# Tile 0's mean from two engines, and small fillers ahead of the first K projection, in a one-core attention and FFN block

## The chip, the core and the metric

The kernel runs on one core of a Trainium2 chip. The metric is the device time in microseconds, the median of a few runs; lower is better.

## The reference

The input x is 2048 x 512 (bf16). Its rows are normalised (layer norm without weights), and two branches are added to x: linear attention with 32 heads of 16 on the normalised rows, and a SwiGLU FFN with F = 1792, on the same normalised rows.

```python
def layernorm(x, eps=1e-5):
    m = jnp.mean(x, axis=-1, keepdims=True)
    v = jnp.var(x, axis=-1, keepdims=True)
    return (x - m) / jnp.sqrt(v + eps)

xn = layernorm(x)
q, k, v = split(xn @ wqkv)                       # 32 heads of 16
phi = lambda t: jnp.where(t > 0, t + 1, jnp.exp(t)) + 1e-6
kv, z = sum_s phi(k) v, sum_s phi(k)             # per head
attn = (phi(q) @ kv) / (phi(q) @ z + 1e-6) @ wo
ffn = (silu(xn @ w_gate) * (xn @ w_up)) @ w_down
out = x + attn + ffn
```

## The kernel before

The 2048 rows are 16 tiles of 128 rows, and each tile lies on the 128 partitions with its 512 columns along the free dimension. A small class keeps one list of instructions per engine: TensorE (PE), ScalarE (ACT), VectorE (DVE), GpSimd (POOL) and the DMA queue of SyncE (SP). Each operation names what it reads and writes, and the class derives the semaphore waits from that. Every engine runs its list strictly in the order in which the program text adds to it, so the order of calls is the schedule, written out by hand.

A phase at the start brings tiles 0 to 3 to TensorE without waiting for the full normalisation. A tile t is centred (its mean subtracted: `xc_half`, `xc_full`), transposed in 128 x 128 blocks by TensorE (`tp_first(t, h, b)`, two blocks for the half h, into PSUM bank b), and copied out by ScalarE (`tc_first`) into `xcT`. The projections take `xcT` (`proj_part(t, "wk", c, pos)`, one matmul over the 128 rows of chunk c, and `proj_first`), and the factor 1/sqrt(var + eps), called `rstd`, comes in afterwards as the scale of the ACT operations that read the projections: `first_ek` (exponential of K), `first_pk` (Relu of K) and `first_pq` (Q). "K 0" is the K projection of tile 0, four matmuls; "K 1" that of tile 1.

The statistics of a tile are `bns` (L297) and `agg` (L300) on DVE, which leave mean and variance in `mv`; `eps` (L325) adds the epsilon and `rstd_of` (L334) raises to the power -1/2 on POOL. For tile 1 the mean comes from ACT instead: `mean_act` (L305) copies the row scaled by 1/512 with a running sum. `xn_dve` (L314) writes the fully normalised tile `xn`, which the accumulation `gtacc` (L569) and later the DMA transposes for tiles from 4 on (`kproj`, `qproj`, L417) need.

`fill(n, cols)` (L269) issues n matmuls of constants into bank 3, which is overwritten later; they compute nothing. The x and wk loads are issued first by SP and ACT: x 0 by SP, x 1 by ACT, wk 0 and 1 together by SP, wk 3 by ACT, wk 2 by SP. K 0 takes its chunks in the order 0, 1, 3, 2.

The rest of the program follows in loops: tiles 5 to 15 of K and Q with their features and `gtacc`, then 56 steps of the FFN (L770) with the attention's normalisation and the output tiles (L942, L953) between them. The waits on which the steps around the change depend can be read in the lines that follow.

Of the kernel before, what the change touches and what calls it, by code (L numbers as in the profile page):

```python
# [6 lines left out]
ACT = mybir.ActivationFunctionType  # L7
ALU = mybir.AluOpType
AX = mybir.AxisListType

P = 128
S = 2048
D = 512
# [95 lines left out]
def bass_parallel_sum__linear_attn_block__swiglu_ffn__prompt_kernel(  # L109
# [12 lines left out]
    K = _Prog()  # L122
    pe, act, dve, pool, sp = nc.tensor, nc.scalar, nc.vector, nc.gpsimd, nc.sync
    bf, f32 = dt.bfloat16, dt.float32

    with contextlib.ExitStack() as es:
        E = es.enter_context

        def sb(name, shape, d=bf):
            return E(nc.sbuf_tensor(name, [P] + shape, d))  # L130

        x_sb = sb("x_sb", [NT, D])
        xn_sb = sb("xn_sb", [NT, D])
        xc_sb = sb("xc_sb", [4, D])
# [12 lines left out]
        mv = sb("mv", [NT, 2], f32)  # L147
        vpe = sb("vpe", [NT], f32)
        rstd = sb("rstd", [NT], f32)
        nb = sb("nb", [NT], f32)  # L150
# [3 lines left out]
        warm = sb("warm", [1], f32)  # L154
        mact = sb("mact", [2, 1], f32)
        scr = sb("scr", [D])
        pkq = sb("pkq", [NT, 2, D])
        zacc = sb("zacc", [D], f32)
        zhi = sb("zhi", [D])
# [30 lines left out]
        def bk(i):  # L190
            return ("bank", i)
# [31 lines left out]
        def whalf(name, dst, src, h):  # L223
# [16 lines left out]
                out=ident[:, :], in_=ident[:, :], compare_op=ALU.not_equal, fill=1.0,  # L240
                base=0, pattern=[[-1, P]], channel_multiplier=1,
            ),
            r=[("ident",)], w=[("ident",)],
# [19 lines left out]
        cx = nc.const_aps.tensor(1.0, (P, 512), bf)  # L263

        def fill(n, cols, after=()):
            K.op(
                "pe",
                [
                    (lambda: pe.matmul(banks[3][:, 0:cols], cw, cx[:, 0:cols], start=True, stop=True))  # L269
                    for _ in range(n)  # L270
                ],
                r=list(after), w=[bk(3)],
            )
# [22 lines left out]
        def bns(t):  # L296
            K.op("dve", lambda: dve.bn_stats(stats[:, t, :], x_sb[:, t, :]), r=[("x", t)], w=[("st", t)])  # L297

        def agg(t):
            K.op("dve", lambda: dve.bn_aggr(mv[:, t, :], stats[:, t, :]), r=[("st", t)], w=[("mv", t)])  # L300

        def mean_act(t):
            K.op(
                "act",
                lambda: act.activation(  # L305
                    scr[:, :], x_sb[:, t, :], ACT.Copy, scale=1.0 / D, accum_out=mact[:, t, :],
                ),
                r=[("x", t)], w=[("mact", t), ("scr",)],
            )

        def xn_dve(t):
            K.op(
                "dve",
                lambda: dve.tensor_scalar(  # L314
                    out=xn_sb[:, t, :], in0=x_sb[:, t, :], scalar1=mv[:, t, 0:1], scalar2=rstd[:, t:t + 1],
                    op0=ALU.subtract, op1=ALU.mult,
                ),
                r=[("x", t), ("mv", t), ("rstd", t)], w=[("xn", t)],
            )

        def eps(t, eng):
            h = dve if eng == "dve" else pool
            K.op(
                eng,
                lambda: h.tensor_scalar(  # L325
                    out=vpe[:, t:t + 1], in0=mv[:, t, 1:2], scalar1=1e-5, scalar2=None, op0=ALU.add,
                ),
                r=[("mv", t)], w=[("vpe", t)],
            )

        def rstd_of(t):
            K.op(
                "pool",
                lambda: pool.tensor_tensor(out=rstd[:, t:t + 1], in0=vpe[:, t:t + 1], in1=nhalf[:, :], op=ALU.pow),  # L334
                r=[("vpe", t), ("nhalf",)], w=[("rstd", t)],
            )
# [15 lines left out]
            )  # L352

        HD = D // 2

        def xc_half(t, h, mean=None, dep="mv"):
            mean = mv[:, t, 0:1] if mean is None else mean

            K.op(
                "dve",  # L360
                lambda: dve.tensor_scalar(
                    out=xc_sb[:, t, h * HD:(h + 1) * HD], in0=x_sb[:, t, h * HD:(h + 1) * HD],
                    scalar1=mean, scalar2=None, op0=ALU.subtract,
                ),
                r=[("x", t), (dep, t)], w=[("xc", t, h)],
            )

        def xc_full(t):
            K.op(
                "dve",  # L370
                lambda: dve.tensor_scalar(
                    out=xc_sb[:, t, :], in0=x_sb[:, t, :], scalar1=mv[:, t, 0:1], scalar2=None, op0=ALU.subtract,
                ),
                r=[("x", t), ("mv", t)], w=[("xc", t, 0), ("xc", t, 1)],
            )
# [8 lines left out]
        def tp_first(t, h, b):  # L384
            tb = banks[b].bitcast(bf)[:, 0:HD].rearrange("p (c s) -> p c s", c=2)
            K.op(
                "pe",
                [
                    (lambda c=c: pe.transpose(  # L389
                        tb[:, c, :], xc_sb[:, t, (2 * h + c) * P:(2 * h + c + 1) * P], ident[:, :],  # L390
                    ))
                    for c in range(2)
                ],
                r=[("xc", t, h), ("ident",)], w=[bk(b)],
            )

        def tc_first(t, h, b):
            tb = banks[b].bitcast(bf)[:, 0:HD].rearrange("p (c s) -> p c s", c=2)
            K.op(
                "act",  # L400
                lambda: act.activation(xcT[:, NDC * t + 2 * h:NDC * t + 2 * h + 2, :], tb, ACT.Copy),
                r=[bk(b)], w=[("xcT", t, h)],
            )
# [36 lines left out]
        def proj_part(t, wname, c, pos):  # L440
            lo, b = (D, kb(t)) if wname == "wk" else (0, qb(t))
            K.op(
                "pe",
                lambda: pe.matmul(  # L444
                    banks[b], xcT[:, NDC * t + c, :], wqkv_sb[:, c, lo:lo + D],
                    start=(pos == 0), stop=(pos == NDC - 1),
                ),
                r=[("xcT", t, c // 2), (wname, c)], w=[bk(b)],
            )

        def kb(t):
            return 2 * (t % 2)

        def qb(t):
            return 2 * (t % 2) + 1
# [49 lines left out]
        def first_pk(t):  # L505
            K.op(
                "act", lambda: act.activation(kpos[:, t % NE, :], banks[kb(t)], ACT.Relu, scale=rstd[:, t:t + 1]),
                r=[bk(kb(t)), ("rstd", t)], w=[("kpos", t % NE)],
            )
# [74 lines left out]
        def xn(t):  # L584
            xn_dve(t)
            if t >= 3:
                transpose_dma(t)

        fill(8, 512)
        bns(0)  # L590
        agg(0)
        xc_half(0, 0)
        xc_half(0, 1)
        mean_act(1)
        xc_half(1, 0, mact[:, 1, :], "mact")
        xc_half(1, 1, mact[:, 1, :], "mact")
        tp_first(0, 0, 4)
        tc_first(0, 0, 4)
        fill(1, P)
        tp_first(0, 1, 5)  # L600
        tc_first(0, 1, 5)
        eps(0, "pool")
        tp_first(1, 0, 6)
        tc_first(1, 0, 6)
        bns(1)
        rstd_of(0)
        xn_dve(0)
        tp_first(1, 1, 7)
        agg(1)
        tc_first(1, 1, 7)  # L610
        bns(2)
        agg(2)
        xc_half(2, 0)
        xc_half(2, 1)
        bns(3)
        agg(3)
        proj_part(0, "wk", 0, 0)
        proj_part(0, "wk", 1, 1)
        proj_part(0, "wk", 3, 2)
        proj_part(0, "wk", 2, 3)  # L620
        first_ek(0)
# [13 lines left out]
        proj_part(0, "wq", 0, 0)  # L635
        proj_part(0, "wq", 1, 1)
        first_pk(0)
        tp_first(2, 0, 4)
        tc_first(2, 0, 4)
        tp_first(2, 1, 5)  # L640
# [26 lines left out]
        xn(4)  # L667
        xload("sp", sp, 12, 2)
        xn_dve(1)
        rstd_of(3)  # L670
        eps(5, "pool")
# [378 lines left out]
```

## Time and profile before

| | us |
|---|---|
| median of 3 runs | 211.25 |
| lowest and highest | 211.05, 211.78 |
| profiled execution, device time | 211.43 |
| its span, first to last instruction | 210.1 |
| PE busy in the span | 206.3 |
| DVE, ACT, POOL busy | 119.6, 70.9, 75.0 |

The profile is of one execution. Its span lies inside the device time, with 1.33 us around it. Lines such as L389 are lines of the kernel; a group's line can be that of a helper that many calls share. PE is TensorE's matmuls and transposes, PEld its weight loads, which overlap matmuls. In a chain of waits each row has a start, a duration, and what ran or what was waited for; in the timeline a row with "xN" is N instructions in a row, from the first one's start to the last one's end.

### The profile page before, as it was taken

The page shows a single profiled execution, that of the slowest core. Times are in us where ns is not written, and L with a number is a line of the kernel's source. Part 1 is how long each engine was busy: PE and PEld are TensorE (multiplying, and loading weights), DVE is VectorE, ACT ScalarE, POOL GpSimd, SP SyncE. Part 2 cuts the span into 40 slices and gives each one's busy share as a digit, 9 for nine tenths or more (in the row PEclk, how much of TensorE's full clock was granted, in tenths as well). Part 3 has the DMA queues.
Part 4 walks back from the last instruction along what each step waited for, and adds up shares of the span by engine and source line. Part 5 has one row for each costly group of instructions (what it writes and reads, how often), then busy time and mean ns, then how long its engine had stood idle before and what let it go on. Part 6 is the DMA issues. An engine that isn't in the chain of part 4 may idle for free.

```text
span 210.1 us, 2753 instructions
## 1 busy us (share of the span) xinstructions
PE 206.3 (98%) x968; PEld 95.3 (45%) x987; DVE 119.6 (57%) x245; ACT 70.9 (34%) x125; POOL 75.0 (36%) x96
## 2 busy tenths in 40 slices
PE   8999999999999999999999999999999999999996
PEld 3444444445444444444444444444444444444444
DVE  3999888335265774647365746365556535374122
ACT  4787666966643331303122312213031213121000
POOL 3667977658032444222140432230424032221200
PEclk9999999999999999999999999999999999999999
DMA  6775444894792011110202110202021010210201
GB/s 196 221 188 122 77 100 100 251 368 156 207 352 48 8 29 27 36 25 28 50 2 50 25 28 25 50 0 50 3 50 25 27 25 28 43 33 27 50 25 53
DMA packets 30287, 16.84 MB, mean 80 GB/s; under 512 B 20928, under 2 KB 29632, under 8 KB 30272
## 3 DMA queue, kind: packets, MB, share of 16 engines
q1 hardware_dynamic: 29984, 16.39, 29.2%
q10 hardware_dynamic: 288, 0.26, 0.4%
q8 instruction: 8, 0.13, 0.3%
q14 instruction: 7, 0.06, 0.1%
HBM read 9.70 MB, written 2.10 MB: 56 GB/s over the span
## 4 chain that ended last, share of the span: by engine, by line
PE 96%; DVE 1%; issue 1%; POOL 1%; DVEq 0%
PE psum L770 44%; PE psum L953 23%; PE psum L417 10%; PE psum L942 7%; PE psum L569 7%; PE psum L444 2%; PE psum L269 2%; PE psum L431 2%; PE psum L389 1%; POOL prod L900 1%; PE psum L868 0%; PE psum L891 0%; DVE pkq L493 0%; DVE den L908 0%; DVE xn_sb L791 0%
## 5 line engine op out<-in xcount | busy, mean ns | idle before, releaser
L785 ACT ACTIVATE sg<-psum 128x512 bf16<-128x512 f32 x56 | 33.4, 598 | 106.8 <-PE psum L770 104.1
L770 PE MATMUL psum<-xnT,wg_sb 128*128 128x512 bf16 x222 | 57.4, 379 | 0.1
L770 PE MATMUL psum<-xnT,wu_sb 128*128 128x512 bf16 x217 | 56.0, 379 | 0.4
L900 POOL TENSOR_TENSOR prod<-pkq,zb 128x512 f32<-128x512 bf16 x16 | 18.6, 1161 | 57.8 <-DVE pkq L493 57.8
L770 PEld LDWEIGHTS psum<-xnT,wu_sb 128*128 128x128 bf16 x224 | 21.9, 98 | 26.4
L770 PEld LDWEIGHTS psum<-xnT,wg_sb 128*128 128x128 bf16 x224 | 21.9, 98 | 26.2
L966 DVE TENSOR_TENSOR out_sb<-psum,x_sb 128x512 bf16<-128x512 f32 (+2 forms) x17 | 11.2, 661 | 36.3 <-PE psum L953 36.3
L924 POOL TENSOR_TENSOR pqn<-pkq,rden 128x512 bf16<-128x512 bf16 x16 | 16.9, 1056 | 36.6 <-DVE rden L918 36.6
L791 DVE TENSOR_TENSOR pkq<-psum,sg 128x512 bf16<-128x512 f32 x28 | 19.2, 687 | 18.5 <-PE psum L770 14.0
L791 DVE TENSOR_TENSOR xn_sb<-psum,sg 128x512 bf16<-128x512 f32 x28 | 18.9, 673 | 13.8 <-PE psum L770 13.2
L953 PE MATMUL psum<-wd_sb,xn_sb 128*128 128x512 bf16 (+2 forms) x123 | 25.4, 355 | 0.2
L953 PE MATMUL psum<-wd_sb,pkq 128*128 128x512 bf16 x110 | 25.2, 379 | 0.1
L417 PE MATMUL psum<-wqkv_sb,xnT 128*128 128x512 bf16 x94 | 22.2, 379 | 0.1
L561 POOL TENSOR_TENSOR zacc<-zacc,pkq 128x512 f32<-128x512 f32 x15 | 17.3, 1156 | 5.0 <-DVE ek L484 4.6
L953 PEld LDWEIGHTS psum<-wd_sb,xn_sb 128*128 128x128 bf16 x126 | 11.8, 98 | 12.5
L953 PEld LDWEIGHTS psum<-wd_sb,pkq 128*128 128x128 bf16 x112 | 11.0, 98 | 13.2
L942 PE MATMUL psum<-m_sb,eq 128*128 128x512 bf16 (+2 forms) x67 | 16.5, 366 | 0.1
L569 PE MATMUL psum<-pkq,xn_sb 128*128 128x512 bf16 x63 | 15.9, 379 | 0.1
L417 PEld LDWEIGHTS psum<-wqkv_sb,xnT 128*128 128x128 bf16 x96 | 9.4, 98 | 11.3
L908 DVE TENSOR_REDUCE den<-prod 128x32 f32<-128x512 f32 x16 | 10.9, 684 | 5.7 <-POOL prod L900 5.7
L297 DVE BATCH_NORM_STATS2 stats<-x_sb 128x6 f32<-128x512 bf16 x16 | 10.9, 681 | 3.2 <-DMA x_sb<-in_A_x_dram 3.2
L493 DVE SCALAR_TENSOR_TENSOR pkq<-pkq,eq 128x512 bf16<-128x512 bf16 x16 | 11.1, 693 | 0.6
(65 smaller groups left out, 142.5 us busy)
## 6 DMA issues: line engine op xcount, KB each, us to landing
out_dram<-out_sb SPq DMA_DIRECT2D x15, 128.0 KB, 1.7
wg_sb<-in_B_w_gate_dram SPq DMA_DIRECT2D x2, 896.0 KB, 7.8
wu_sb<-in_B_w_up_dram SPq DMA_DIRECT2D x2, 896.0 KB, 6.0
wd_sb<-in_B_w_down_dram SPq DMA_DIRECT2D x1, 1792.0 KB, 9.7
x_sb<-in_A_x_dram SPq DMA_DIRECT2D x5, 256.0 KB, 3.0
x_sb<-in_A_x_dram SPq DMA_DIRECT2D x5, 128.0 KB, 3.5
wqkv_sb<-in_A_wqkv_dram SPq DMA_DIRECT2D x5, 128.0 KB, 3.6
wqkv_sb<-in_A_wqkv_dram SPq DMA_DIRECT2D x1, 512.0 KB, 7.9
```

The costliest lines, as they stand in the source:

```text
L417: (lambda c=c: pe.matmul(banks[b], xnT[:, c, t * P:(t + 1) * P], wqkv_sb[:, c, lo:lo + D], start=(c == 0), stop=(c == NDC - 1),))
L493: lambda: dve.scalar_tensor_tensor(out=dst, in0=src, scalar=0.0, in1=e, op0=ALU.max, op1=ALU.add,),
L561: lambda: pool.tensor_tensor(out=zacc[:, :], in0=zacc[:, :], in1=pk, op=ALU.add),
L569: (lambda c=c: pe.matmul(banks[4 + c], xn_sb[:, t, c * P:(c + 1) * P], pkq[:, t, 0, :], start=(t == 0), stop=(t == NT - 1),))
L770: (lambda c=c: pe.matmul(banks[b], w_sb[:, c, fc * P:(fc + 1) * P], xnT[:, c, C * 512:(C + 1) * 512], start=(c == 0), stop=(c == NDC - 1),))
L785: lambda: act.activation(sg[:, j % NSG, :], banks[gb], ACT.Silu),
L791: lambda: dve.tensor_tensor(out=hT(C, fc), in0=banks[ub], in1=sg[:, j % NSG, :], op=ALU.mult,),
L900: lambda: pool.tensor_tensor(out=p, in0=pkq[:, t, 1, :], in1=zb[:, :], op=ALU.mult),
L924: lambda: pool.tensor_tensor(out=pqn[:, t % NPN, :].rearrange("p (h e) -> p h e", e=DH), in0=pkq[:, t, 1, :].rearrange("p (h e) -> p h e", ...
L942: (lambda g=g: pe.matmul(dst, pqnT(t)[:, g, :], m_sb[:, g, lo:hi], start=(g == 0), stop=False,))
L953: (lambda fc=fc: pe.matmul(dst, hT(C, fc)[:, jj * P:(jj + 1) * P], wd_sb[:, fc, lo:hi], start=False, stop=(fc == NFC - 1),))
L966: lambda: dve.tensor_tensor(out=o, in0=src, in1=x_sb[:, t, lo:hi], op=ALU.add),
```

## The change

Tile 0's mean no longer comes from `bns` and `agg`. `mean_parts(0)` sums the first 256 columns on DVE (a multiply by ones with a sum) and the other 256 on ACT, each scaled by 1/512, and `xc_two` subtracts both parts in one DVE instruction with two scalars. `bns(0)` follows the centring of tile 0, and `agg(0)`, `eps(0)` (now on DVE), `rstd_of(0)` and a new `negmean(0)` on POOL (minus mean times rstd) follow the centring of tile 1. Tile 0 is normalised on ACT (`xn_act(0)`) behind `first_pk(0)`, in place of `xn_dve(0)` on DVE.

On PE, the eight fillers of 512 columns become seven and one of 128. The filler of 128 columns between tile 0's two transposes goes away, and four of 128 stand behind them. Tile 1's transposes move from ahead of K 0 to between its second and third matmul. Tile 2 is centred in one instruction instead of two halves.

```diff
+        scr2 = sb("scr2", [D // 2])
+        mpart = sb("mpart", [2], f32)
...
+        def negmean(t):
+            K.op(
+                "pool",
+                lambda: pool.tensor_scalar(
+                    out=nb[:, t:t + 1], in0=mv[:, t, 0:1], scalar1=rstd[:, t:t + 1], scalar2=-1.0,
+                    op0=ALU.mult, op1=ALU.mult,
+                ),
+                r=[("mv", t), ("rstd", t)], w=[("nb", t)],
+            )
+
+        def xn_act(t):
+            K.op(
+                "act",
+                lambda: act.activation(
+                    xn_sb[:, t, :], x_sb[:, t, :], ACT.Identity, scale=rstd[:, t:t + 1], bias=nb[:, t:t + 1],
+                ),
+                r=[("x", t), ("nb", t), ("rstd", t)], w=[("xn", t)],
+            )
...
+        def mean_parts(t):
+            K.op(
+                "dve",
+                lambda: dve.tensor_tensor_reduce(
+                    out=scr2[:, :], in0=x_sb[:, t, 0:HD], in1=cx[:, 0:HD], scale=1.0 / D, scalar=0.0,
+                    op0=ALU.mult, op1=ALU.add, accum_out=mpart[:, 0:1],
+                ),
+                r=[("x", t)], w=[("mpa", t), ("scr2",)],
+            )
+            K.op(
+                "act",
+                lambda: act.activation(
+                    scr[:, 0:HD], x_sb[:, t, HD:D], ACT.Copy, scale=1.0 / D, accum_out=mpart[:, 1:2],
+                ),
+                r=[("x", t)], w=[("mpb", t), ("scr",)],
+            )
+
+        def xc_two(t, h):
+            K.op(
+                "dve",
+                lambda: dve.tensor_scalar(
+                    out=xc_sb[:, t, h * HD:(h + 1) * HD], in0=x_sb[:, t, h * HD:(h + 1) * HD],
+                    scalar1=mpart[:, 0:1], scalar2=mpart[:, 1:2], op0=ALU.subtract, op1=ALU.subtract,
+                ),
+                r=[("x", t), ("mpa", t), ("mpb", t)], w=[("xc", t, h)],
+            )
...
-        fill(8, 512)
+        fill(7, 512)
+        fill(1, P)
+        mean_parts(0)
+        mean_act(1)
+        xc_two(0, 0)
+        xc_two(0, 1)
         bns(0)
-        agg(0)
-        xc_half(0, 0)
-        xc_half(0, 1)
-        mean_act(1)
         xc_half(1, 0, mact[:, 1, :], "mact")
         xc_half(1, 1, mact[:, 1, :], "mact")
+        agg(0)
+        eps(0, "dve")
+        rstd_of(0)
+        negmean(0)
         tp_first(0, 0, 4)
         tc_first(0, 0, 4)
-        fill(1, P)
         tp_first(0, 1, 5)
         tc_first(0, 1, 5)
-        eps(0, "pool")
-        tp_first(1, 0, 6)
-        tc_first(1, 0, 6)
+        fill(4, P)
         bns(1)
-        rstd_of(0)
-        xn_dve(0)
-        tp_first(1, 1, 7)
         agg(1)
-        tc_first(1, 1, 7)
         bns(2)
         agg(2)
-        xc_half(2, 0)
-        xc_half(2, 1)
+        xc_full(2)
         bns(3)
         agg(3)
         proj_part(0, "wk", 0, 0)
         proj_part(0, "wk", 1, 1)
+        tp_first(1, 0, 6)
+        tc_first(1, 0, 6)
+        tp_first(1, 1, 7)
+        tc_first(1, 1, 7)
         proj_part(0, "wk", 3, 2)
         proj_part(0, "wk", 2, 3)
         first_ek(0)
...
         proj_part(0, "wq", 0, 0)
         proj_part(0, "wq", 1, 1)
         first_pk(0)
+        xn_act(0)
         tp_first(2, 0, 4)
```

## The prediction

> **What bounds the kernel now.** I read the page's first part, then the chain of waits for the first 18 us, because every line of the diff lies there.
>
> ```profile
> PE 206.3 (98%) x968; PEld 95.3 (45%) x987; DVE 119.6 (57%) x245; ACT 70.9 (34%) x125; POOL 75.0 (36%) x96
> ...
> PE 96%; DVE 1%; issue 1%; POOL 1%; DVEq 0%
> ```
>
> TensorE is busy 206.3 of 210.1 us and carries 96% of the chain. So an edit ahead of K 0 changes the end only by the moment from which PE has dense work, by pauses it opens after that moment, and by the rate of the matmuls.
>
> ```profile
> 0.84 3.57 PE psum L269 x8
> 4.41 0.03 issue
> 4.44 0.40 PE psum L389 x2
> 4.84 0.11 PE psum L269
> 4.94 0.64 PE psum L389 x6
> 5.58 2.90 PE psum L444 x12
> 8.48 0.22 PE psum L389 x4
> 8.71 0.86 PE psum L444 x4
> ```
>
> The chain (start, us, what) has eight filler matmuls (L269), tile 0's first two transposes at 4.44 (L389), one small filler, six more transposes, then the projections (L444). From 4.44 on there is no pause: the transposes of tile 1 fill the time in which tile 0's transposed halves are copied out and the weights land.
>
> ```profile
> 3.15 0.69 DVE L297 BATCH_NORM_STATS2 stats<-x_sb 128x6 f32<-128x512 bf16 x1 [3.15 <-DMA x_sb<-in_A_x_dram]
> 3.45 0.63 ACT L305 ACTIVATE scr<-x_sb 128x512 bf16<-128x512 bf16 x1 [1.16 <-DMA x_sb<-in_A_x_dram]
> 3.88 0.18 DVE L300 BATCH_NORM_AGGREGATE mv<-stats 128x2 f32<-128x6 f32 x1
> 3.99 0.19 ACT L305 ACTIVATION_READ_ACCUMULATOR scr<-x_sb 128x1 f32 x1
> 4.10 0.48 DVE L361 TENSOR_SCALAR xc_sb<-x_sb,mv 128x256 bf16<-128x256 bf16 x2
> 4.87 1.25 ACT L401 ACTIVATE xcT<-psum 128x256 bf16<-128x256 bf16 x4 [0.70 <-PE psum L389]
> 5.38 1.17 PE L444 MATMUL psum<-wqkv_sb,xcT 128*128 128x512 bf16 x3
> 6.60 1.03 PE L444 MATMUL psum<-wqkv_sb,xcT 128*128 128x512 bf16 x4
> ```
>
> The timeline gives tile 0's path: its load at 3.15, statistics, aggregate, centring, transposes, copies, K 0 at 5.38. The last two rows show the rate: eight fillers start (3.57 - 0.63) / 7 = 0.42 us apart, the four matmuls from 6.60 start (1.03 - 0.38) / 3 = 0.217 apart. K 0's three starts are 5.38, 5.80 and 6.16; the second gap of 0.36 splits into 0.42 and 0.217 rates at about 6.1 us. So up to 6.1 us PE runs at half rate. (PEclk is 9 in all slices, so this is not in the granted clock's row.)
>
> The landing rows of the wk transfers, for the one issued at 1.26 by SP and the one at 1.35 by ACT:
>
> ```profile
> DMA to landing us min/median/max: 3.8/3.8/3.8
> DMA to landing us min/median/max: 3.8/4.0/4.3
> ```
>
> wk 0 and 1 are there at 1.26 + 3.8 = 5.06, wk 3 at 1.35 + 4.3 = 5.65. K 0 can't start before 5.06, whatever tile 0 does. At most 5.38 - 5.06 = 0.32 us is to be had at K 0's start.
>
> **The change part by part.**
>
> *Tile 0's mean.* Statistics, aggregate and wait take 4.10 - 3.15 = 0.95 us to the first centring. Now ACT sums one half: its 128x512 row is 0.63 with the read starting 0.54 after it; the 128x256 ACT row (L401) is 0.38, so the read starts about 0.32 after 3.15 and takes 0.19: 3.66. DVE's half is an operation that the trace does not have. Bounds: not under a 256-wide TENSOR_SCALAR (0.28), and not over the 512-wide statistics plus a read of an accumulator as on ACT (0.69 + 0.19 = 0.88). I take 0.45, nearer the low end, because it passes half as many elements as the 0.69 row. Then mpart is complete at 3.66, and the first centring starts at 3.70 instead of 4.10. With a second scalar it is dearer: the 512-wide rows are 0.40 with two (L314) and 0.35 with one (L371), so 0.28 + 0.05 = 0.33 each. Halves done at 4.05 and 4.29, before at 4.38 and 4.58.
>
> *Tile 0's transposes and copies.* Before, a copy started 4.87 - 4.44 = 0.43 after the first transpose. Now 4.10 + 0.43 = 4.53 and 4.35 + 0.45 = 4.80; ACT is free, since mean_act(1) waits for the read at 3.66 (it writes the same scr) and ends near 3.70 + 0.73 = 4.43. Each copy takes 0.38: halves 4.91 and 5.19. K 0's first matmul: the wk landing 5.06 plus a weight load, about 5.15, 0.22 earlier than 5.38. At the upper bound of DVE's half, the first centring starts at 4.07, K 0 again near 5.38, and this gain is nothing. The four small fillers behind tile 0's transposes need 4 x 0.107 = 0.43 (the chain's one is 0.11), 4.56 to 4.98, inside the wait for wk. They cost nothing there; at the upper bound they still end by 5.35.
>
> *Tile 1's transposes leave the wait and go behind K 0's first pair.* That is what costs. Before, they were done in time that had nothing else in it. Now four transposes, 0.107 each at half rate and 0.055 at full (the chain's 0.22 for 4 at 8.48), stand in dense work. K 0's pair goes 5.15 to 6.00; the transposes 6.00 to 6.27 with the step at 6.1; K 0's second pair starts 6.27 and ends 6.70, where before K 1 started at 6.60. wk 3 (5.65) is long there. Net so far: +0.10.
>
> *K 1 now waits for ACT.* Its first matmul needs tile 1's first half: transposes at 6.00 and 6.10, copy from about 6.37 to 6.75, weight load, matmul near 6.87. Between none (full rate earlier) and 0.3 (half rate, copies late) I take 0.15. Net: K 1 at 6.85 instead of 6.60, +0.25.
>
> *DVE, POOL, xn 0.* bns(0) now stands ahead of tile 1's centring (ready near 5.26, needed at 6.00), and agg(0), eps(0) behind it. rstd(0) needs 5.35 + 0.05 + 0.14 + 0.65 (L334 row), about 6.2; first_ek(0) needs it near 6.92, so 0.7 covers it. negmean on POOL (0.32, the L325 row) delays rstd(2) by at most that, and its first reader, first_ek(2), is at 11.69, rstd(2) at 8.03. Removing xn_dve(0) takes 0.31 from DVE ahead of bns(2), which waited for its transfer to 6.06 anyway; later DVE steps come about 0.2 later and feed xc 3's transposing DMA (from 8.78 to about 9.0, landing 2.5 later, PE needs it at 11.9) and xn 1, 2. xn_act(0) on ACT is 0.63 behind first_pk(0), 8.1 to 8.7. Queued behind it is the copy of tile 2, which in the old order starts at 8.63 and here no sooner than 8.9, because PE is late by 0.25. Without that cover it would cost up to 0.5. gtacc(0) needs xn 0 at 11.1. All at nothing.
>
> *Sum.* K 0's start -0.22, transposes and their place +0.32, K 1's wait +0.15: +0.25 us, carried by dense PE work to the end. The profiled execution took 211.43 (span 210.1, 1.33 around it), 0.18 over the median 211.25. So 211.68 against the former, **211.5** against the latter.
>
> **A rule on the rate.** In the trace the rate steps up at 6.1 us, 5.25 us after the first filler and 1.7 after the last pause (4.41). [...]
>
> **The rivals.**
>
> *The rate steps up later (slower).* The new order has up to three pauses ahead of K 0, near 3.95 to 4.10, 4.2 to 4.3 and 4.98 to 5.15, where the old has 0.03. If the step counts from the last pause, it comes at 5.15 + 1.7 = 6.85: 0.75 x (1 - 0.217 / 0.42) = +0.36, so 211.9. If dense work must start anew, 5.15 + 5.25 = 10.4: 4.3 x 0.48 = +2.1, so 213.6. Against it: PE stays over 85% busy there. It decides over 0.3% from a step at 6.9 on. [...]
>
> *K 0's start is the end's start (faster).* If tile 1's transposes cover a wait for wk 3, and ACT's copies come in time, the gain of 0.22 to 0.32 stays: 210.95 to 211.05. For it speaks only that wk landings vary; here c 3 waited for nothing at 6.16.
>
> *The rate steps up earlier (faster).* At K 0's start, 5.15 rather than 6.1: 0.95 x 0.48 = -0.46, 211.05. To be 0.3% faster it must come before tile 0's transposes, which no row suggests.
>
> *It does nothing measurable.* DVE's half sum is so slow, or wk so late, that PE's order alone decides: 211.25.
>
> **How the numbers follow.** Forecast (+0.1 to +0.5) 0.5, nothing 0.1, faster start 0.1, late step 0.24 (0.1 of it by a whole window or more), early step or a saving I don't see 0.06. A measurement of this kernel tells about 0.3%, 0.63 us, from no change; the three runs alone spread 0.73. Slower beyond that takes most of the late step and the upper ends of the forecast: 0.26. Faster: the last case and part of the faster start: 0.11. Range 210.7 to 212.6: it leaves out the dear end of the late step and the far faster end. The likeliest case alone: 211.3 to 211.8.
>
> **What would show it.** Right: centring from 3.7, K 0's first matmul at 5.1 to 5.2, four transposes between K 0's pairs, K 1 near 6.85 with a weight load released by ACT xcT, nothing new behind 9 us. Wrong: matmul starts 0.42 apart beyond 6.9, DVE's half sum over 0.9 us, K 1 before 6.6, or a pause of PE behind xn_act(0).

## The result, and the profile after

The changed kernel took 211.44 us (median of 22 runs, 210.95 to 211.91), the kernel before, run beside it, 210.99 (22 runs, 210.82 to 211.78). The ratio of the two is 1.0018 with a 95% interval of 1.0010 to 1.0025: 0.2% slower, less than 0.3%, and real. The profiled execution of the changed kernel took 211.51 with a span of 210.3; before's was 211.43 with 210.1.

The page's first part and its chain of waits answer to the first lines of the prediction:

```profile
PE 207.3 (99%) x990; PEld 95.0 (45%) x990; DVE 119.4 (57%) x246; ACT 72.0 (34%) x128; POOL 75.5 (36%) x96
...
PE 90%; POOL 4%; DVE 3%; DMA 1%; issue 1%; ACT 0%; DVEq 0%; POOLq 0%
```

The busy time of PE can't be compared closely, since the trace of before lacks 19 of its 987 matmul records (its weight loads are all there, 987, and the new order has three fillers more). The chain can: PE carried 96% of it, now 90, and POOL and DVE hold 7%. Something on those two engines has come onto the path: the chain now leaves PE at a wait near 20 us and follows POOL and DVE back from there. The 7% is the length of that stretch, not what the change costs.

The timeline of tile 0's path (start, duration, engine, line, operation, and in brackets the engine's idle time before it):

```profile
3.35 0.42 ACT L388 ACTIVATE scr<-x_sb 128x256 bf16<-128x256 bf16 x1 [1.06 <-DMA x_sb<-in_A_x_dram]
3.35 0.43 DVE L380 CUSTOM_DVE_ANT_0 scr<-x_sb,const-bfloat16-1.0 128x256 bf16<-128x256 bf16 x1 [3.35 <-DMA x_sb<-in_A_x_dram]
...
3.67 0.19 ACT L388 ACTIVATION_READ_ACCUMULATOR scr<-x_sb 128x1 f32 x1
3.70 0.08 DVE L380 DVE_READ_ACCUMULATOR2_ANT mpart<- 128x1 f32 x1
...
3.90 0.60 DVE L397 TENSOR_SCALAR xc_sb<-x_sb,mpart 128x256 bf16<-128x256 bf16 x2
...
5.17 0.61 PE L492 MATMUL psum<-wqkv_sb,xcT 128*128 128x512 bf16 x2
...
5.62 0.39 PE L437 MATMUL psum<-ident,xc_sb 128*128 128x128 bf16 x4
...
5.84 1.35 PE L492 MATMUL psum<-wqkv_sb,xcT 128*128 128x512 bf16 x5
...
6.36 0.11 PEld L492 LDWEIGHTS psum<-wqkv_sb,xcT 128*128 128x128 bf16 x2 [0.42 <-ACT xcT L449]
```

The load landed at 3.35, 0.2 later than in the trace of before. Both half sums start then, and the centring follows 0.55 later (before 0.95). K 0's first pair starts at 5.17 and 5.40, tile 1's transposes stand behind it at 5.62, and K 1 starts at 6.37, 0.095 late for ACT's copy (the gap to it is 0.311 where 0.216 is the spacing). The rate has stepped up by 5.17: the last small fillers were still 0.107 apart, the transposes are 0.056 apart. In the trace of before it stepped at 6.1.

So at 6.4 us this execution is 0.23 *ahead* of before's profile, and it stays 0.22 ahead up to 16.7. Then PE pauses twice, here in its timeline:

```profile
16.53 0.59 PE L465 MATMUL psum<-wqkv_sb,xnT 128*128 128x512 bf16 x2
17.11 1.04 PE L617 MATMUL psum<-pkq,xn_sb 128*128 128x512 bf16 x4
17.98 1.89 PE L465 MATMUL psum<-wqkv_sb,xnT 128*128 128x512 bf16 x8
19.98 0.39 PE L617 MATMUL psum<-pkq,xn_sb 128*128 128x512 bf16 x1
```

L617 is `gtacc`. `gtacc(3)` starts at 17.11, 0.366 after the matmul before it, a pause of 0.15. `gtacc(4)` starts at 19.98, 0.27 late. The two take 0.42, the lead of 0.22 becomes a lag of 0.2, and that holds to the end. The list of PEld's waits from 6 to 30 us names what was late (total, times, longest):

```profile
PEld psum L617 <- DVE pkq L541: 0.6, 1, 0.6
PEld psum L492 <- ACT xcT L449: 0.6, 2, 0.4
PEld psum L617 <- DVE xn_sb L335: 0.5, 1, 0.5
```

The DVE rows that it points to, from the timeline of DVE:

```profile
16.65 0.41 DVE L335 TENSOR_SCALAR xn_sb<-x_sb,mv,rstd 128x512 bf16<-128x512 bf16 x1
...
19.24 0.68 DVE L541 SCALAR_TENSOR_TENSOR pkq<-psum,ek 128x512 bf16<-128x512 f32 x1
```

The same two in the trace of before:

```profile
15.88 0.41 DVE L314 TENSOR_SCALAR xn_sb<-x_sb,mv,rstd 128x512 bf16<-128x512 bf16 x1
...
18.48 0.68 DVE L493 SCALAR_TENSOR_TENSOR pkq<-psum,ek 128x512 bf16<-128x512 f32 x1
```

They start at 15.88 and 18.48: DVE is 0.77 late. Going back along DVE's list, it had stood idle twice for POOL:

```profile
14.45 0.41 DVE L335 TENSOR_SCALAR xn_sb<-x_sb,mv,rstd 128x512 bf16<-128x512 bf16 x1 [0.46 <-POOL rstd L355]
15.32 0.41 DVE L335 TENSOR_SCALAR xn_sb<-x_sb,mv,rstd 128x512 bf16<-128x512 bf16 x1 [0.46 <-POOL rstd L355]
```

POOL's rows for tile 5's `eps` and `rstd`, of the changed kernel and then of the kernel before:

```profile
12.00 1.14 POOL L346 TENSOR_SCALAR vpe<-mv 128x1 f32<-128x1 f32 x1
13.22 1.19 POOL L355 TENSOR_TENSOR rstd<-vpe,nhalf 128x1 f32<-128x1 f32 x1
```

```profile
11.37 0.22 POOL L325 TENSOR_SCALAR vpe<-mv 128x1 f32<-128x1 f32 x1
11.68 0.57 POOL L334 TENSOR_TENSOR rstd<-vpe,nhalf 128x1 f32<-128x1 f32 x1
```

POOL's whole chain is later (`eps(2)` at 7.46 for 7.06, its feature product at 9.46 for 8.88), and then `eps(5)`, 0.22 before, took 1.14. This is a chain that the prediction put at nothing.

### The profile page after: what moved, and what is told of

It is laid out like the page before. It is cut to its first block, busy times and chain, and to the rows that moved or that the text cites. A ratio compares the mean times of both kernels' runs of the same rounds, so it can differ in the third digit from the quotient of the medians.

```text
span 210.3 us, 2785 instructions
## 1 busy us (share of the span) xinstructions
PE 207.3 (99%) x990; PEld 95.0 (45%) x990; DVE 119.4 (57%) x246; ACT 72.0 (34%) x128; POOL 75.5 (36%) x96
## 4 chain that ended last, share of the span: by engine, by line
PE 90%; POOL 4%; DVE 3%; DMA 1%; issue 1%; ACT 0%; DVEq 0%; POOLq 0%
PE psum L820 46%; PE psum L1003 23%; PE psum L465 8%; PE psum L992 7%; PE psum L617 5%; POOL rstd L355 2%; DMA x_sb<-in_A_x_dram 1%; POOL vpe L346 1%; DVE stats L299 1%; POOL pkq L574 1%; PE psum L918 0%; PE psum L941 0%; DVE xn_sb L335 0%; DVE pkq L541 0%; DVE pkq L581 0%
## 5 line engine op out<-in xcount | busy, mean ns | idle before, releaser
L820 PE MATMUL psum<-xnT,wu_sb 128*128 128x512 bf16 x224 | 57.5, 379 | 0.0
L617 PE MATMUL psum<-pkq,xn_sb 128*128 128x512 bf16 x64 | 16.0, 379 | 0.1
L355 POOL TENSOR_TENSOR rstd<-vpe,nhalf 128x1 f32<-128x1 f32 x16 | 10.0, 627 | 5.4 <-DVE vpe L346 4.2
```

The costliest lines, as they stand in the source:

```text
L617: (lambda c=c: pe.matmul(banks[4 + c], xn_sb[:, t, c * P:(c + 1) * P], pkq[:, t, 0, :], start=(t == 0), stop=(t == NT - 1),))
L820: (lambda c=c: pe.matmul(banks[b], w_sb[:, c, fc * P:(fc + 1) * P], xnT[:, c, C * 512:(C + 1) * 512], start=(c == 0), stop=(c == NDC - 1),))
```

## The experiments

Theory 1: the order on DVE delays the statistics, POOL's chain comes late, and PE waits at `gtacc`. Theory 2: PE's own order costs the time (tile 1's transposes in dense work, K 1 behind ACT's copy). Beside both stands the moment of the rate step, which differed by 0.95 us between the two profiles.

**The kernel before, again** (unchanged).

> The kernel before, unchanged, for a second profile of it. Theory 1 (POOL): the 22 runs of before lie mostly at 210.8 to 211.1, below the profiled one at 211.43, so this execution should take about 211.0 and its matmul rate should step up before 6.1 us, near 5.2 as in the changed kernel's profile; K 1 then starts near 6.1 instead of 6.60, and TensorE has no new pause up to 25 us. Theory 2 (the order on TensorE): the step comes at 6.1 again, K 1 at 6.60, 211.4.

211.55 in a single execution, beside a median of 210.94 for 29 others of the same kernel. The step came at 6.5, K 1 at 6.85, no pause behind it. The early step that was expected did not come; the step moves from execution to execution of one kernel (6.1 in the first profile, 6.5 here).

**Tile 5's and 6's `eps` taken from POOL** (changed kernel).

```diff
 bns(6)
 agg(6)
+eps(5, "dve")
+eps(6, "dve")
...
 rstd_of(3)
-eps(5, "pool")
 rstd_of(5)
-eps(6, "pool")
 rstd_of(6)
```

> The changed kernel with the two small steps eps(5) and eps(6) on VectorE (0.14 us each) instead of POOL, where eps(5) took 1.14 us in the changed kernel's profile. Theory 1: what the change costs is a late POOL chain (rstd 5 and 6 late, so xn 5 and xn 6, so tile 3's features, so TensorE's waits of 0.15 and 0.27 us at gtacc(3) and gtacc(4)); taking the 1.14 us step away gives 0.25 to 0.45 back: 211.0 to 211.2, and the two waits go. Theory 2: the cost is tile 1's transposes behind K 0 and K 1's wait for ACT, which stay: 211.4, as the changed kernel.

211.32 (12 runs), ratio to before 1.0010 (1.0000 to 1.0021). Neither pause at `gtacc` is in the trace. That alone doesn't show that the edit took them away: tile 0's load was on time here (3.13), and the second profile of the changed kernel itself, with such a load (the last run below), has no such pause either. And its profile took 211.47, because another pause of 0.63 stands at tile 7's K projection:

```profile
23.42 0.81 PE L465 MATMUL psum<-wqkv_sb,xnT 128*128 128x512 bf16 x3 [0.47 <-DMA xnT<-xn_sb]
```

The DMA that transposes tile 7's `xn` needed 5.0 us to land; in most other executions it took 2.4 to 3.8.

**Only PE's part of the change** (kernel before).

```diff
-fill(8, 512)
+fill(7, 512)
+fill(1, P)
...
-fill(1, P)
 tp_first(0, 1, 5)
 tc_first(0, 1, 5)
+fill(4, P)
-tp_first(1, 0, 6); tc_first(1, 0, 6); tp_first(1, 1, 7); tc_first(1, 1, 7)
...
 proj_part(0, "wk", 1, 1)
+tp_first(1, 0, 6); tc_first(1, 0, 6); tp_first(1, 1, 7); tc_first(1, 1, 7)
 proj_part(0, "wk", 3, 2)
```

> The kernel before with TensorE's part of the change alone: seven fillers and a small one, no filler between tile 0's transposes, four small ones behind them, tile 1's transposes between K 0's second and third matmul. Mean, statistics and normalisation stay as before. Theory 1: 211.0, at most 211.1, since POOL and VectorE are untouched. Theory 2: K 1 waits for ACT's copy and tile 1's transposes are in dense work, +0.25: 211.2 to 211.3.

211.42 (12 runs), ratio 1.0019 (1.0007 to 1.0031): without the earlier K 0, PE's order alone costs about as much as the whole change, within this interval. Its timeline and its list of waits:

```profile
5.47 0.60 PE L444 MATMUL psum<-wqkv_sb,xcT 128*128 128x512 bf16 x2
5.92 0.39 PE L389 MATMUL psum<-ident,xc_sb 128*128 128x128 bf16 x4
6.14 1.35 PE L444 MATMUL psum<-wqkv_sb,xcT 128*128 128x512 bf16 x5
```

```profile
PEld psum L444 <- ACT xcT L401: 0.6, 2, 0.4
```

K 0 to K 1 is 1.19 us (5.47 to 6.67), with 0.096 of it K 1's wait, and there is no later pause. K 0 itself is at 5.47, with its load 0.16 later than in before's first profile. Theory 2 is right about its part. (K 0 to K 1 is 0.88 in the old order at full rate, as a run below shows.)

**POOL late without the rest** (kernel before, two spare 128x1 multiplies on POOL that nothing reads).

```diff
 first_pq(0)
+spare(2)
+spare(2)
 eps(2, "pool")
```

> The kernel before with two spare 128x1 operations on POOL ahead of eps(2), which nothing reads: POOL's chain of small steps runs some 0.6 us later, as in the changed kernel, and nothing else is changed. Theory 1: the same collision and the same waits at gtacc(3) and gtacc(4): +0.3 to +0.5, 211.3 to 211.5. Theory 2: POOL has slack, 211.0.

211.29 (12 runs), ratio 1.0011 (0.9999 to 1.0023). In the trace tile 3's features are 0.59 late, PE pauses by 0.12 at `gtacc(0)` and 0.10 at `gtacc(4)`, not at `gtacc(3)`:

```profile
PEld psum L579 <- POOL pkq L536: 0.5, 1, 0.5
PEld psum L579 <- DVE pkq L503: 0.4, 1, 0.4
```

A later POOL chain alone opens pauses of this kind, smaller than the 0.3 to 0.5 that was expected; its effect on the time can't be told from none by this interval.

**Tile 1's transposes back ahead of K 0** (changed kernel).

```diff
+xc_half(1, 0, ...); xc_half(1, 1, ...)
 bns(0)
-xc_half(1, 0, ...); xc_half(1, 1, ...)
 agg(0)
...
 tc_first(0, 1, 5)
-fill(4, P)
+tp_first(1, 0, 6); tc_first(1, 0, 6); tp_first(1, 1, 7); tc_first(1, 1, 7)
...
 proj_part(0, "wk", 1, 1)
-tp_first(1, 0, 6); tc_first(1, 0, 6); tp_first(1, 1, 7); tc_first(1, 1, 7)
```

> The changed kernel with tile 1's four transposes back ahead of K 0 (and its centring ahead of bns(0), so that they are ready in time); the four small fillers behind tile 0's transposes make way for them. Theory 2 (the order on TensorE): K 0 to K 1 again in 0.86 us instead of 1.20, so -0.3 against the changed kernel: 211.1 or less. Theory 1 (late statistics and POOL): statistics come 0.3 later still than in the changed kernel, and waits at gtacc(3) and gtacc(4) take back what K 0 gains: 211.4.

211.41 (9 runs) beside 211.10 of before (27 runs), ratio 1.0017 (1.0007 to 1.0026). K 1 does come earlier, at 5.95, but PE then pauses by 0.29 at 7.46 for tile 2's centring on DVE, by 0.23 at 11.44, and by 0.28 at tile 7's K projection. The gain is given back.

**The same, and `eps` 5 and 6 on DVE** (the diff above and that of tile 5's and 6's `eps`).

> The same, and eps(5) and eps(6) on VectorE as before in the study. If both theories hold, each for a part, this one loses neither: 210.8 to 210.9, the fastest so far. Theory 2 alone: as the run without this edit. Theory 1 alone: as the changed kernel with eps(5), eps(6) moved, 211.3.

211.25 (11 runs), 1.0010 (1.0001 to 1.0020). K 1 at 5.77; pauses of 0.31, 0.22 and 0.10, the first again for tile 2's centring:

```profile
PEld psum L437 <- DVE xc_sb L419: 0.6, 1, 0.6
```

**Tile 0 normalised on DVE again** (changed kernel).

```diff
 rstd_of(0)
-negmean(0)
...
 bns(1)
+xn_dve(0)
 agg(1)
...
 first_pk(0)
-xn_act(0)
```

> The changed kernel with tile 0 normalised on VectorE as before (xn_dve(0) ahead of agg(1), no negmean, no xn_act). Theory 1: VectorE's statistics get 0.3 us later, POOL's chain with them, and TensorE's waits at gtacc(3), gtacc(4) grow: 211.6 to 211.8. Theory 2: TensorE's order is the changed kernel's, 211.4.

211.64 (5 runs, 211.52 to 212.04), ratio 1.0033 (1.0021 to 1.0045), the dearest of all. The load is on time here (3.13); one more row of 0.41 on DVE ahead of tile 2's statistics makes tile 3's features 0.88 late, `eps(5)` on POOL takes 1.14 again, and PE's list of waits begins with the three lines of the changed kernel's first profile, word for word:

```profile
PEld psum L617 <- DVE pkq L541: 0.6, 1, 0.6
PEld psum L492 <- ACT xcT L449: 0.6, 2, 0.4
PEld psum L617 <- DVE xn_sb L335: 0.5, 1, 0.5
```

Theory 1's mechanism is shown: later statistics, the same two pauses (0.21 and 0.27), and a longer time in the median. And `xn_act` seems to be a part of the change that helps (1.0018 with it against 1.0033, with intervals that just overlap).

**No small fillers** (changed kernel without its `fill(1, P)` and `fill(4, P)`).

> The changed kernel without any small filler (the one behind the seven and the four ahead of K 0). If the small fillers hold the time at which the matmul rate steps up, as the rival of a later step has it, the step moves behind 6.9 us in some runs and the median goes up by 0.3 or more, 211.8. If they only fill a pause: 211.4, with the same spread as the changed kernel, 210.95 to 211.9.

Median 211.41 (12 runs), ratio 1.0025 (1.0003 to 1.0047), but two of the 12, which widen this interval, took 213.16 and 213.40. No run of any other kernel here, some 230 in all, was over 212.04. The profiled execution is one of the usual ones:

```profile
4.10 0.65 PE L437 MATMUL psum<-ident,xc_sb 128*128 128x128 bf16 x4
4.97 1.04 PE L492 MATMUL psum<-wqkv_sb,xcT 128*128 128x512 bf16 x2 [0.22 <-ACT xcT L449]
5.80 0.63 PE L437 MATMUL psum<-ident,xc_sb 128*128 128x128 bf16 x4
6.22 1.15 PE L492 MATMUL psum<-wqkv_sb,xcT 128*128 128x512 bf16 x4
```

Here K 0's pair is 0.40 apart and the transposes 0.107: half rate up to 6.3. The two dear runs left no trace; their 1.7 to 2.0 us over the median are near the 2.1 at which the prediction priced a rate step that has to start anew.

**Relieved order** (changed kernel; `eps` 5 and 6 on DVE in their old places, tile 2's statistics and centring ahead of tile 1's statistics).

```diff
-eps(5, "pool")
+eps(5, "dve")
...
-eps(6, "pool")
+eps(6, "dve")
...
-bns(1); agg(1)
 bns(2); agg(2)
 xc_full(2)
+bns(1); agg(1)
```

> The changed kernel with its order on TensorE, but with eps(5) and eps(6) on VectorE where they stand, and tile 2's statistics and centring ahead of tile 1's statistics. Theory 1 (late statistics and POOL are the whole cost): the waits at gtacc(3) and gtacc(4) go and the time is that of before, 211.0. Theory 2 (the order on TensorE costs by itself): tile 1's transposes and K 1's wait of 0.1 stay, 211.2 to 211.3. Both: between the changed kernel and before.

211.36 (12 runs) beside 210.92 of before (29 runs), ratio 1.0013 (1.0000 to 1.0027). No pause at `gtacc` is in its trace (the load was on time here too, 3.12); PE pauses by 0.26 at 11.42 for K 3, and by 0.60 at 22.90, tile 7's DMA landing in 4.8.

**Best version that the runs pointed to** (relieved, and tile 1's transposes ahead of K 0 in place of the four small fillers).

> The same, with tile 1's transposes back ahead of K 0 and its centring ahead of bns(0): tile 0's mean in halves and xn_act(0) are what is left of the change, with nothing of either cost. In the run a_tp_back_eps TensorE still paused 0.3 us for tile 2's centring; with tile 2's statistics first that goes. Theory 1 and theory 2 together: 210.75 to 210.95, 0.05 to 0.2 under before, from K 0's earlier start. If a pause remains elsewhere: 211.2.

211.16 (12 runs), ratio 1.0008 (0.9996 to 1.0020). It doesn't beat the kernel before. Two pauses remain, 0.18 at K 2 and 0.29 at K 3:

```profile
PEld psum L479 <- ACT xcT L449: 0.7, 2, 0.5
PEld psum L479 <- ACT kpos L555: 0.6, 1, 0.6
```

**The kernel before with `eps` 5 and 6 on DVE** (the four `eps` lines of the relieved diff alone).

> The kernel before with eps(5) and eps(6) on VectorE where they stand, as a control of what that edit is worth by itself. Theory 1: before has slack on POOL, so no difference, 211.0. If POOL limits before too in its faster runs: 210.8.

210.88 (12 runs), ratio 0.9995 (0.9983 to 1.0008): no difference, which fits that nothing of PE waits for POOL in the traces of before. Its profile, 210.82, is the undisturbed case of the old order, with the step no later than 4.5. K 0 starts at 5.21, ten matmuls follow each other, and K 1 is at 6.09:

```profile
5.21 2.33 PE L444 MATMUL psum<-wqkv_sb,xcT 128*128 128x512 bf16 x10
```

**The changed kernel, again** (unchanged).

> The changed kernel, unchanged, for a second profile of it: in the first, tile 0's load came 0.2 us later than in before's. Theory 1: VectorE's statistics of tile 2 are 0.2 to 0.3 later than before's by the new order alone, and if the rate steps up before 5.5 us, TensorE waits again for tile 3's features (gtacc(3), gtacc(4)) or for a transposing DMA, 0.2 us or more in sum. If the waits came only from the late load, there is none here and the time is under 211.2 with an early step.

210.86, beside 211.03 of before. PE's and POOL's rows:

```profile
4.96 0.60 PE L492 MATMUL psum<-wqkv_sb,xcT 128*128 128x512 bf16 x2
5.40 0.39 PE L437 MATMUL psum<-ident,xc_sb 128*128 128x128 bf16 x4
5.62 1.56 PE L492 MATMUL psum<-wqkv_sb,xcT 128*128 128x512 bf16 x6
```

```profile
11.57 0.29 POOL L346 TENSOR_SCALAR vpe<-mv 128x1 f32<-128x1 f32 x1
11.95 1.39 POOL L355 TENSOR_TENSOR rstd<-vpe,nhalf 128x1 f32<-128x1 f32 x1
```

The load landed 0.2 earlier than in the first profile. `eps(5)` took 0.29, but `rstd(5)` 1.39; it ended at 13.34 instead of 14.41, and tile 3's features are 0.07 later than in before's trace instead of 0.76. No pause at `gtacc`. So between these two executions 0.2 at the load goes with 0.7 at the features.

## Why the prediction was right, and where it was not

Each profiled time can be put together from two readings: how much later K 1 starts than the 6.09 of the undisturbed old order (210.82), and PE's pauses behind it (each gap less 0.216).

| kernel | K 1 later | pauses behind | sum | time less 210.82 |
|---|---|---|---|---|
| before, first profile | 0.51 | 0 | 0.51 | 0.61 |
| before, again | 0.76 | 0 | 0.76 | 0.73 |
| only PE's part | 0.58 | 0 | 0.58 | 0.55 |
| POOL late | 0.32 | 0.22 | 0.54 | 0.60 |
| no small fillers | 0.69 | 0 | 0.69 | 0.64 |
| changed, again | 0.06 | 0 | 0.06 | 0.04 |
| changed, first profile | 0.28 | 0.42 | 0.70 | 0.69 |
| `eps` 5, 6 on DVE | 0.06 | 0.63 | 0.69 | 0.65 |
| tile 0 on DVE again | 0.27 | 0.48 | 0.75 | 0.82 |
| transposes back | -0.14 | 0.80 | 0.66 | 0.63 |
| transposes back, `eps` on DVE | -0.32 | 0.63 | 0.31 | 0.28 |
| relieved | 0.13 | 0.86 | 0.99 | 0.96 |
| best | -0.04 | 0.46 | 0.42 | 0.40 |

The sums agree with the times to 0.1, most to 0.05. So nothing else over 0.1 is needed, and every pause counts in full to the end, as the prediction had it from the chain's 96% of PE. The first column isn't the edit's alone: it holds the landing of the load and the moment of the rate step of that execution as well.

*Tile 0's mean: right.* DVE's half, its read of 0.08 included, was done 0.43 after the load (forecast 0.45), the centring came 0.55 after the load (forecast 0.55).

*K 0's start -0.22: right in size.* With early steps on both sides it is 4.97 for 5.21, -0.24 (the two kernels with `eps` 5 and 6 on DVE in place). The wk landing that the forecast took as the bound (5.06) was at 4.57 in the changed kernel's first profile, so it was no longer the bound there; K 0 followed the last small filler directly (5.07 to 5.17). That the size came out all the same is luck in part.

*Tile 1's transposes +0.32 and K 1's wait +0.15: right in kind, large in size.* K 0 to K 1 is 1.19 in the new order and 0.88 in the old, both at full rate: 0.32 for the two together, of which the wait is 0.095. The forecast's 0.47 reckoned with the step at 6.1, and so with part of this at half rate. With K 0's -0.24 the net is +0.06 to +0.08 (K 1 at 6.15 for 6.09, in executions with an early step), not +0.25. K 1 at 6.37 and 6.15 lies before 6.6, which the prediction had named as a sign of being wrong.

*"DVE, POOL, xn 0 ... All at nothing": this step failed.* It saw that later DVE steps come about 0.2 later, and checked tile 3's transposing DMA and `xn` 1 and 2 as their readers, but not that the same delay passes through POOL's list to `rstd(5)`, on which DVE stands while tile 3's features, one `xn` and tile 4's features queue behind. In the first profile this cost 0.42, in the second nothing. With DVE's list later still it costs 0.48 at the same two places even with the load on time (tile 0 on DVE again). "Nothing new behind 9 us", named as a sign of being right, failed with it.

*The sum, +0.25 against +0.45 measured.* That the forecast of 211.5 lies so near is luck in part. Two deviations stand against each other: PE's part was cheaper by about 0.2, the statistics dearer. And its base of 211.25 was the median of three runs, while all 22, these three among them, have 210.99. By PE's part alone, +0.06 to +0.08, the change would be hard to see; the rest of the 0.45 must come from pauses like those at `gtacc`, or from executions in which load and rate step fall otherwise. How often each occurs in the 22 runs can't be read, since only profiled executions leave a trace; so the 0.45 is not split exactly. What is shown is that PE's order takes back K 0's gain, and that the pauses come on top in some executions.

*The rivals.* A later rate step is not seen in either profile of the changed kernel (about 5.15 and 4.9). The runs without small fillers would fit that rival: leave the fillers out, and 2 of 12 lie 1.75 and 1.99 us over the median, where the prediction's estimate, from the trace's 5.25 us between first filler and step, has 2.1 for dense work that must start anew. That the step was late in these two, and that they are no accident of another kind, isn't shown. The chances speak of "a whole window"; no run shows such a window, only the moments of the step. The early step, at K 0's start or just before it, did happen in both profiles, but it happens in the old order as well (the kernel before with `eps` 5 and 6 on DVE), so it favours neither. In these traces the step lay anywhere from about 4.1 to 6.5 us, a range of 2.4; what sets its moment isn't shown. In the old order this, with the load, accounts for the spread that the traces show (K 1 at 6.09, 6.60 and 6.85 in 210.82, 211.43 and 211.55); the two profiles of the changed kernel, 0.65 apart, differ by 0.22 at K 1, which is the load, and by the 0.42 of pauses.

*Taking away one wait at a time* didn't beat the kernel before. With the `gtacc` waits gone, the next pause stood at tile 7's DMA or at K 3; with the transposes back, at tile 2's centring. What stays open is why tile 7's DMA needed 4.3 to 5.0 us in three executions. The traces have a lead: beside the data queues, the profile has packets of the kind "instruction" on queues 8 and 14 (15 in the changed kernel's first profile). In five executions none of these started between this DMA's issue and its last 0.1 us, and it took 2.4 to 2.7; in seven one did, and it took 3.0 to 4.3; in two executions two did, and it took 4.8 and 5.0. Other transposing DMAs with such a packet beside them took as little as 2.5, and that the packets are the cause wasn't tried.

## What to carry to other kernels

When an edit shortens a wait ahead of the critical engine's dense work, look for what had its place in that wait: here transposes that had filled it went into dense work, and 0.32 us went back where K 0 had gained 0.24. When an edit puts an engine 0.2 us behind, follow the delay through every queue to the last reader and not only to the first, since an in-order engine that stands for one late operand holds all that is queued behind it (here DVE stood twice for 0.46 us, and tile 3's features came 0.76 late). Compare profiles only after events whose moment differs from execution to execution (here the rate step and the first load) have been read in both, or what they move (up to 0.76 us at K 1 here) will be taken for the edit's.

## What of the hardware was unexpected

- The step in the matmul rate (starts of 512 columns from 0.42 to 0.216 us apart) came at about 4.1 to 6.5 us in 14 executions of 12 kernels, at 6.1 and 6.5 in two executions of the same one.
- A 128x1 addition on POOL took 0.22 us in one execution and 1.14 in another, with DVE busy throughout both, and a 128x1 power 0.55 to 1.39; the trace doesn't show what they waited for.
- The sum on DVE over 128x256 (L380) took 0.43 us and its accumulator's read 0.08, where the read on ACT took 0.19.
- The transposing DMA of tile 7 (128x512) landed in 2.4 to 3.8 us in 11 executions and in 4.3, 4.8 and 5.0 in three; during the two longest two packets of the kind "instruction" started, during the five shortest none before the last 0.1 us.
